# GpSimd additions ordered behind VectorE's port passes, later Q projections and two more weight buffers in a fused two-layer transformer kernel

## The chip, the cores and the metric

The kernel runs on one core of a Trainium2 chip. The metric is the device time of one execution in microseconds (us); lower is better. The engines are TensorE (PE in the profile, with its weight loads as PEld), VectorE (DVE), ScalarE (ACT), GpSimd (POOL) and SyncE (SP), which issues the DMAs.

## The reference

Two identical blocks follow each other, each with its own attention and its own dense part, on x of 2048 rows by 512 columns in bf16. Every matrix is the same in both blocks.

```python
def _A_ref(x, wqkv, wo):                      # 32 heads of 16 columns
    q, k, v = split(x @ wqkv)                 # [H, 2048, 16] each
    p = softmax(einsum("hqd,hkd->hqk", q, k) * 16 ** -0.5)
    return concat(einsum("hqk,hkd->hqd", p, v)) @ wo
def _B_ref(x, w1, b1, w2, b2):                # 512 -> 1792 -> 512
    return gelu(x @ w1 + b1) @ w2 + b2
for _ in range(2):
    x = x + _A_ref(layernorm(x), wqkv, wo)
    x = x + _B_ref(layernorm(x), w1, b1, w2, b2)
```

The softmax's 32 x 2048 x 2048 exponentials per layer are the bulk of the elementwise work.

## The kernel before, in words

Rows are cut into four chunks of 512 queries (the last chunk of layer 1 into two segments of 256). A *pass* is one group of four heads of one chunk over a range of the 16 key tiles of 128 rows. Its unit is a *cell*: the scores of one head's 512 columns against one key tile, [128, 512] in one PSUM bank. There are 4096 cells in the two layers.

A cell's exponential is taken in one of two ways. Most go to ScalarE (`exps`, L1751): one ACTIVATE with Exp reads two or three neighbouring banks (two or three cells) and writes bf16 units called `pt`, which lie in the ring of that name or in lent tensors (`kt`, `q`, `v`, `g`). The others, only for the key tiles listed in `KD`, go over VectorE and GpSimd (`join`, `dfirst`, `dchain`). VectorE evicts the bank with one TENSOR_SCALAR that turns the score into the bits of a bf16 power of two (L1507, into a `du` buffer, of which some lie in `kt` and `v`). GpSimd then makes three shifted copies by adding integers to those words: L1596 makes copy 1, L1598 copies 2 and 3, for one or two cells at once. The four copies are multiplied by V and by three scaled copies of V (`vc`, L1282), so that such a cell takes four products where ScalarE's takes one. `pvs` (L1817) does all these products.

Around the attention run, per chunk, the output projection (`wo`), a layernorm, the dense part (`hpair`, `gelu`, `ytile`), another layernorm, and the next layer's K, V and Q projections (`proj`, spawned by `projections`). A layernorm (`ln`, `ln_tile`) consists of statistics per tile, a row of very small VectorE instructions on [128, 1] to [128, 4] columns (VARR L739, RSTD L749 and L755, RA L752, RB L753, NMR L757), which form the inverse square root, and one pass per tile (XLN, L774). Q is masked per head pair into `qp` (L1299); the softmax division writes `ott` (L946).

Weights come in pieces of 256 KB into a pool of buffers `WR` (`wloads`, `wload`, L1035): four of its own, and for the last segment four more in layer 0's K (`wlate`). Every piece's buffer comes free when its last use is ordered, and the next load in a fixed list takes it. SyncE issues all DMAs in order.

Nothing is ordered by hand. `_Sched` runs all these generators against planned clocks of the engines and writes out one instruction list per engine; on the chip the lists run in order and semaphores keep the dependencies. The planner chooses, at each step, the ready operation with the earliest start. `_ready` adds one thing to the dependencies: an operation marked `port` (a VectorE instruction that reads and writes SBUF) is not planned to start inside a GpSimd addition, and the other way round. In the kernel before this is only in the planned times, and the mark is set by the name of what is written:

```python
self.port = eng == "dve" and ... self.writes[0].startswith(("OTT", "NMR", "QP", "VC", "XLN", "PT", "V0", "V1")) ...
if op.eng == "pool":
    at = max(t, self.clock["pool"])
    for a, b in self.port_ops[-4:]:
        if a <= at < b - HEAD:
            at = t = b - HEAD
```

When TensorE would wait, the planner fills in dummy matmuls (`filler`, L1339, and the zero products at L1825). `PICKS` chooses for each stretch of 24 planned microseconds one of the rows of constants in `ORDERS`, by which the planner decides.

Of the kernel before, what the change touches and what calls it, by code (L numbers as in the profile page):

```python
# [50 lines left out]
KD = ((4, 5, 6, 7, 8), (0, 1, 2, 8, 12))  # L51
NKD = 5
TAIL = 10
OPENING = 18
# [46 lines left out]
STRETCH = 24  # L101
PICKS = (3, 9, 9, 3, 3, 3, 9, 3, 1, 3, 3, 9, 9, 9, 1, 9, 9, 3, 9, 9, 5, 3, 3, 9,
         3, 9, 9, 9, 3, 1, 9, 9, 3, 9, 9, 9, 3, 3, 9, 3, 9, 3, 9, 9, 3, 5, 9, 5,
         1, 9, 9, 9, 9, 3, 9, 9, 5, 3, 4, 3)
LOG2E = 1.4426950408889634
# [114 lines left out]
class _Op:  # L220
    __slots__ = ("eng", "cost", "fns", "reads", "writes", "sem", "by", "tail", "prio", "mode", "slack", "late", "back", "port", "limit", "after")

    def __init__(self, eng, cost, fns, reads=(), writes=(), sem=None, by=1, tail=0.0, prio=None, mode="F", slack=None):
        self.eng, self.cost = eng, cost
        self.fns = fns if isinstance(fns, list) else [fns]
        self.reads, self.writes = list(reads), list(writes)
        self.sem, self.by, self.tail, self.prio, self.mode, self.slack = sem, by, tail, prio, mode, slack
        self.limit = 1e9
        self.late, self.after = None, []
        self.port = eng == "dve" and self.writes[:1] != [] and self.writes[0].startswith(("OTT", "NMR", "QP", "VC", "XLN", "PT", "V0", "V1")) and not self.reads[:1] == [] and not self.reads[0].startswith("B.")  # L230

# [19 lines left out]
class _Sched:  # L251
# [152 lines left out]
    def run(self):  # L404
        while True:
# [65 lines left out]
            if e == "dve" and op.port:  # L471
                self.port_ops.append((start, start + cost))
            if e == "pool" and op.writes[0] != "LIB":
                self.pool_ops.append((start, start + cost))


SW = 0.107
STEP = 0.01
DENSITY = {"S": 1.0, "P": 1.0, "F": 4.0}


def bass_interleave_layers__mha_block__dense_activation_gelu__prompt_kernel(
# [15 lines left out]
    with ExitStack() as es:  # L498
# [28 lines left out]
        if DU % 2:  # L527
# [30 lines left out]
        sem_names = ["pe", "act", "dve", "pool", "dxt0", "dxt1", "dxt2", "dxt3", "dx1", "dx2", "dx3", "dwq", "dwk", "dwv", "db1", "db2"] + ["dw%d" % c for c in range(3)] + [  # L558
                     "dout", "dk0", "dk1"] + ["dwr%d" % i for i in range(W_RING + W_MORE)] + ["dtr%d" % i for i in range(XLN_RING)]
        sems = {n: es.enter_context(nc.semaphore("s_" + n)) for n in sem_names}  # L560
# [36 lines left out]
class _Plan:  # L597
# [279 lines left out]
    def projections(self, l, c, prio):  # L877
# [115 lines left out]
    def wloads(self):  # L993
# [33 lines left out]
        for i, (piece, (src, n), uses) in enumerate(out):  # L1027
            if i == len(out) - (NFC // 2 + 1 - W_MORE):
                yield ("spawn", self.wlate(late), 3)
            w = yield ("acq", "w")  # L1030
            yield from self.wload(piece, src, n, uses, w, [])

    def wload(self, piece, src, n, uses, w, over):
# [424 lines left out]
    def scores(self):  # L1458
        u = 0
        pools = self.s.pools  # L1460
        while True:
# [25 lines left out]
            for d, b, pair, j in extra:  # L1487
                yield ("spawn", self.dfirst(pair, j, b), DPRIO)
                if j == 0:
# [14 lines left out]

    def dfirst(self, pair, j, b):
        u = self.T["DU"][pair["du"]][:, 0, j, :]
        yield _Op("dve", 0.682, lambda e: e.tensor_scalar(u, self.bank(b), E_SCALE, E_BIAS, op0=ALU.mult, op1=ALU.add),  # L1507
                  reads=["B.%d" % b], writes=["DU.%d.0.%d" % (pair["du"], j)] + self.over(pair["du"]))
        pair["done"] = pair.get("done", 0) + 1
        yield ("rel", "dbank", b)  # L1510

    def solo(self):
# [10 lines left out]
        while True:  # L1523
# [9 lines left out]
            d, b, pair, j = extra[0]  # L1533
            yield ("spawn", self.dfirst(pair, j, b), DPRIO)
            if j == 0:
# [42 lines left out]
    def dchain(self, pair):  # L1578
# [8 lines left out]
        yield ("cond", lambda: pair.get("done", 0) == len(cells))  # L1587
        n = len(cells)
        U = T["DU"][du]
        key = [["DU.%d.%d.%d" % (du, i, j) for j in range(n)] for i in range(4)]  # L1590
        def words(i, k):
# [4 lines left out]
        yield _Op("pool", 0.151 + 0.2176 * n, lambda e: e.int64_add(words(1, 1), words(0, 1), SHIFT * ONES),  # L1596
                  reads=key[0], writes=key[1])
        yield _Op("pool", 0.143 + 0.4352 * n, lambda e: e.int64_add(words(2, 2), words(0, 2), 2 * SHIFT * ONES),  # L1598
                  reads=key[0] + key[1], writes=key[2] + key[3])
        self.chains -= 1  # L1600
        self.duleft[du] = n
        for jj, (pi, kt, a) in enumerate(cells):
            l, seg, g = self.pas[pi][:3]
            gb, ts = self.heads(seg, g)
            j = KD[l].index(kt)
            for i in range(4):
                if i == 0:
                    ws, wk = [T["V"][l][:, kt, 8 * gb + 2 * a + t, 0:17] for t in ts], ["V%d.%d" % (l, kt), self.vone(l, kt)]
                else:
                    ws = [T["VC"][:, j, i - 1, 17 * h:17 * h + 17] for h in [8 * gb + 2 * a + t for t in ts]]  # L1610
                    wk = ["VC.%d.%d" % (j, i - 1)]
                self.dq[(pi, a)].append((ws, U[:, i, jj, :].bitcast(BF16), wk + [key[i][jj]],
                                         ("du", du) if i == 3 else None, i == 3, kt))

# [246 lines left out]
    def run(self):  # L1861
# [16 lines left out]
        s.spawn(self.loads(), 2)  # L1878
        s.spawn(self.init(), 3)
        s.spawn(self.wloads(), 3)  # L1880
        s.spawn(self.scores(), 0)
# [45 lines left out]
```

## Time and profile before

| | us |
|---|---|
| runs (three) | 1480.62, 1482.77, 1484.39 |
| median | 1482.77 |
| profiled execution, its own time | 1478.68 |
| span of the profile | 1476.7 |
| granted TensorE clock, mean | 0.999 |

| engine | busy us | share of the span | instructions |
|---|---|---|---|
| ACT | 1427.6 | 97% | 1422 |
| PE | 1415.5 | 96% | 19639 |
| DVE | 1219.1 | 83% | 2246 |
| POOL | 977.8 | 66% | 1235 |

The profile is of one execution. Busy time counts an instruction from its recorded start to its end; instructions that follow each other on ACT or DVE overlap in the record, so the mean of one is longer than its share of the busy time. PE's busy time holds the dummy matmuls. The span is 2.0 us shorter than the execution's own time, and that execution was 4.1 us faster than the median.

### The profile page before, as it was taken

Reading aid. Unit: us, or ns where it says so; the run is one execution under the profiler, and the core shown is the slowest. Engines: PE = TensorE matmul, PEld = TensorE weight load, DVE = VectorE, ACT = ScalarE, POOL = GpSimd, SP = SyncE. Lnnn points to the kernel's source line nnn. Section 1 sums busy time; section 2 is a strip of 40 time slices with the busy share of each in tenths; the row PEclk is TensorE's granted clock in tenths of the full one; section 3 lists DMA queues with packets and bytes.
Section 4 is the critical chain, followed back from the end, with each engine's and each line's share of the span. In section 5 each row is a group of like instructions: output and inputs, shape, how many; then the busy total and the mean of one; then the engine's idle time right before and its main releaser. Section 6 shows DMA issues by size and latency. Waiting matters only on the chain.

```text
span 1476.7 us, 45759 instructions
## 1 busy us (share of the span) xinstructions
PE 1415.5 (96%) x19639; PEld 428.0 (29%) x19639; DVE 1219.1 (83%) x2246; ACT 1427.6 (97%) x1422; POOL 977.8 (66%) x1235
## 2 busy tenths in 40 slices
PE   8999999999999999999999999999999999999999
PEld 3222222222222222222222222222222222334445
DVE  7768989878987789987797788999968987887683
ACT  7999999999999999999999999999999999999995
POOL 1057977867676777886556756667867876776661
PEclk9999999999999999999999999999999999999999
DMA  5200001153112521114320243101143115511533
GB/s 154 49 2 1 2 16 30 38 168 82 47 45 59 164 66 31 48 34 130 122 60 25 59 122 114 30 2 37 30 131 115 37 37 137 158 31 38 162 91 95
DMA packets 145045, 103.35 MB, mean 70 GB/s; under 512 B 37069, under 2 KB 143822, under 8 KB 144846
## 3 DMA queue, kind: packets, MB, share of 16 engines
q1 hardware_dynamic: 144846, 100.44, 24.6%
q8 instruction: 157, 2.57, 0.8%
q14 instruction: 42, 0.34, 0.1%
HBM read 88.61 MB, written 4.19 MB: 63 GB/s over the span
## 4 chain that ended last, share of the span: by engine, by line
ACT 52%; PE 30%; DVE 14%; DMA 1%; POOL 1%; issue 1%; SPq 0%; ACTq 0%; DVEq 0%
ACT pt L1751 41%; PE ps L607 10%; PE ps L1351 10%; PE ps L1817 9%; DVE du L1507 6%; ACT g L1102 3%; ACT kt L1751 2%; ACT q L1751 2%; ACT v L1751 2%; DVE kt L1507 1%; DVE v L1507 1%; DVE xln L774 1%; DVE stats L734 1%; DMA wr<-in_B_w_dram 1%; ACT L1102 1%
## 5 line engine op out<-in xcount | busy, mean ns | idle before, releaser
L1751 ACT ACTIVATE pt<-ps 128x1024 bf16<-128x1024 f32 (+1 forms) x1096 | 1103.9, 1136 | 18.2 <-PE ps L1351 12.0
L1507 DVE TENSOR_SCALAR du<-ps 128x512 uint16<-128x512 f32 x858 | 572.4, 683 | 115.9 <-PE ps L1351 112.3
L1351 PE MATMUL ps<-qp,kt 32*128 32x512 bf16 x4096 | 553.8, 384 | 37.4 <-ACT pt L1751 11.4
L1596 POOL INT64_ADD du<-du x444 | 266.9, 602 | 318.5 <-DVE du L1507 290.9
L1598 POOL INT64_ADD du<-du x444 | 449.1, 1013 | 35.5
L1817 PE MATMUL ps<-du,vc 128*17 128x512 bf16 (+1 forms) x2856 | 324.2, 360 | 1.4 <-ACT pt L1751 0.5
L1351 PEld LDWEIGHTS ps<-qp,kt 32*128 32x128 bf16 x4096 | 144.7, 91 | 601.3 <-issue 175.0
L1817 PE MATMUL ps<-pt,v 128*17 128x512 bf16 (+1 forms) x2630 | 283.9, 360 | 5.3 <-ACT pt L1751 2.1
L1507 DVE TENSOR_SCALAR kt<-ps 128x512 uint16<-128x512 f32 x200 | 134.7, 682 | 34.0 <-PE ps L1351 33.2
L1817 PE MATMUL ps<-du,v 128*17 128x512 bf16 (+1 forms) x952 | 142.4, 360 | 3.9 <-DVE xt L937 1.2
L1817 PE MATMUL ps<-kt,vc 128*17 128x512 bf16 (+1 forms) x714 | 136.3, 347 | 0.1
L607 PE MATMUL ps<-xf,wr 128*32 128x512 bf16 (+1 forms) x1888 | 131.0, 365 | 0.0
L607 PE MATMUL ps<-wr,g 128*32 128x512 bf16 x1600 | 118.9, 382 | 1.6 <-DMA wr<-in_B_w_dram 1.5
L1598 POOL INT64_ADD kt<-kt x104 | 105.1, 1011 | 8.3
L1817 PEld LDWEIGHTS ps<-du,vc 128*17 128x17 bf16 x2856 | 87.7, 89 | 75.3 <-issue 38.1
L1596 POOL INT64_ADD kt<-kt x104 | 62.4, 600 | 60.8 <-DVE kt L1507 57.4
L1817 PEld LDWEIGHTS ps<-pt,v 128*17 128x17 bf16 x2630 | 69.1, 88 | 87.7 <-issue 62.5
L1817 PE MATMUL ps<-v,vc 128*17 128x512 bf16 (+1 forms) x402 | 90.3, 350 | 0.0
L1081 DVE TENSOR_SCALAR g<-ps,hb1t 128x512 bf16<-128x512 f32 (+1 forms) x112 | 79.2, 708 | 12.7 <-PE ps L607 12.0
L1817 PE MATMUL ps<-kt,v 128*17 128x512 bf16 (+1 forms) x390 | 85.9, 360 | 1.6 <-DVE xt L937 1.3
L1507 DVE TENSOR_SCALAR v<-ps 128x512 uint16<-128x512 f32 x115 | 77.5, 682 | 11.9 <-PE ps L1351 11.6
L1751 ACT ACTIVATE kt<-ps 128x1024 bf16<-128x1024 f32 (+1 forms) x71 | 78.5, 1134 | 2.5 <-PE ps L1351 0.6
(108 smaller groups left out, 1555.4 us busy)
## 6 DMA issues: line engine op xcount, KB each, us to landing
wr<-in_B_w_dram SPq DMA_DIRECT2D x256, 256.0 KB, 2.9
wr<-in_A_wqkv_dram SPq DMA_DIRECT2D x24, 256.0 KB, 2.9
wr<-in_A_wo_dram SPq DMA_DIRECT2D x18, 256.0 KB, 3.1
x<-in_A_x_dram SPq DMA_DIRECT2D x7, 512.0 KB, 4.1
kept<-x SPq DMA_DIRECT2D x4, 512.0 KB, 2.9
x<-kept SPq DMA_DIRECT2D x4, 512.0 KB, 4.1
out_dram<-x SPq DMA_DIRECT2D x16, 128.0 KB, 2.6
g<-in_A_wqkv_dram SPq DMA_DIRECT2D x3, 512.0 KB, 6.0
```

The source lines that it names most:

```text
L607: return [lambda e, a=a: e.matmul(out[32 * a:32 * a + 32, :], lhsT=lhsT[:, 32 * a:32 * a + 32], rhs=rhs, start=start, stop=stop, tile_posi ...
L734: yield _Op("dve", 0.66, lambda e, t=t: e.bn_stats(T["STATS"][:, t, :], T["X"][:, t % XT, :]), reads=["X.%d" % (t % XT)], writes=["ST.%d" ...
L774: yield _Op("dve", 0.41, lambda e: e.tensor_scalar(xl, T["X"][:, t % XT, :], T["RSTD"][:, t:t + 1], T["NMR"][:, t:t + 1], op0=ALU.mult, op ...
L1081: yield _Op("dve", 0.21 + n / 966, lambda e, fc=fc, pb=pb: e.tensor_scalar(T["G"][:, fc, q], pb, T["HB1T"][:, fc:fc + 1], None, op0=ALU.ad ...
L1102: lambda e, g=g: e.activation(out=g, in_=g, func=ACT.Gelu_apprx_tanh), reads=gk, writes=gk, prio=2)
L1351: return (lambda e: e.matmul(o, lhsT=lhsT, rhs=rhs, start=True, stop=True, tile_position=(32 * a, 0)), ["K%d.%d.%d" % (l, gb, kt // 4), "Q ...
L1507: yield _Op("dve", 0.682, lambda e: e.tensor_scalar(u, self.bank(b), E_SCALE, E_BIAS, op0=ALU.mult, op1=ALU.add), reads=["B.%d" % b], writ ...
L1596: yield _Op("pool", 0.151 + 0.2176 * n, lambda e: e.int64_add(words(1, 1), words(0, 1), SHIFT * ONES), reads=key[0], writes=key[1])
L1598: yield _Op("pool", 0.143 + 0.4352 * n, lambda e: e.int64_add(words(2, 2), words(0, 2), 2 * SHIFT * ONES), reads=key[0] + key[1], writes=k ...
L1751: yield _Op("act", 0.065 + 0.4267 * n, lambda e, src=src, dst=dst: e.activation(out=dst, in_=src, func=ACT.Exp, scale=0.25), reads=["B.%d" ...
L1817: op.fns.append(lambda e, o=o, lhsT=q[0][0][m], rhs=q[0][1][:, n * m:n * m + n], a=a, st=st, sp=sp: e.matmul(o, lhsT=lhsT, rhs=rhs, start= ...
```

## The change

The change has four parts, and a fifth that the description leaves out.

1. The mark `port` is also set for VARR, RSTD, RA and RB. GpSimd's operations are planned behind the newest port pass that is planned to start no later than they do (`last`), and the GpSimd instruction now also waits on the chip, by semaphore, for that pass.
2. In layer 0 the Q projections of chunks 1, 2 and 3 are not spawned before 200, 240 and 280 cells have been scored, and each of a chunk's four eight cells after the one before.
3. `XP`, the transposed input of layer 1's projections, becomes two more weight buffers when the last of these projections is done. In `wlate` only the first piece carries the list of what it overwrites.
4. `PICKS` is another list, so that the whole order is another.
5. The products of a `du` cell are offered copy by copy: copy 0 when its eviction is ordered, the others when their addition is, where all four were offered after both additions.

```diff
-PICKS = (3, 9, 9, 3, 3, 3, 9, 3, 1, 3, 3, 9, ...
+PICKS = (3, 3, 3, 3, 3, 3, 3, 3, 3, 3, 3, 3, ...
+QAT = (0, 200, 240, 280)
+QSTEP = 8
...
-        self.port = ... startswith(("OTT", "NMR", "QP", "VC", "XLN", "PT", "V0", "V1")) ...
+        self.port = ... startswith(("OTT", "NMR", "QP", "VC", "XLN", "PT", "V0", "V1", "VARR", "RSTD", "RA", "RB")) ...
...
         if op.eng == "pool":
-            at = max(t, self.clock["pool"])
-            for a, b in self.port_ops[-4:]:
-                if a <= at < b - HEAD:
-                    at = t = b - HEAD
+            t = max(t, self.last(max(t, self.clock["pool"]))[0])
...
+    def last(self, at):
+        for a, b, ev in self.port_ops[:-9:-1]:
+            if a <= at + LEAN:                       # LEAN = 0.0
+                return b + LATENCY["dve"], ev
+        return 0.0, None
...
+            if e == "pool" and op.writes[0] != "LIB":
+                over = self.last(start)[1]
+                if over:
+                    self.P.wait("pool", *over)
             ev = self.P.group(e, op.fns, op.reads, op.writes, op.sem, op.by)
...
+        T["WR"] += [T["XP"][:, 2 * i:2 * i + 2, :].rearrange("p c f -> p (c f)") for i in range(2)]
...
+            if l == 0 and kind == "Q" and c > 0:
+                yield ("cond", lambda i=i: self.scored >= QAT[c] + QSTEP * i)
             yield ("spawn", self.proj(l, kind, i, c, src, skeys, ph, (kind, l, i, c)), p)
...
+    def wmore(self):
+        self.wover = {}
+        yield ("need", ("pfree", 0, self.segs[0][-1]))
+        for w in (W_RING + W_MORE, W_RING + W_MORE + 1):
+            self.wover[w] = ["XP.%d" % t for t in range(4)]
+            yield ("rel", "w", w)
...
-            yield from self.wload(piece, src, n, uses, W_RING + i, over)
+            yield from self.wload(piece, src, n, uses, W_RING + i, [] if i else over)
...
 # dfirst: after the eviction        self.copied(cell, pair["du"], j, 0)
 # dchain: after the first addition  self.copied(cells[jj], du, jj, 1)
 #         after the second          self.copied(cells[jj], du, jj, i)   for i in (2, 3)
+    def copied(self, cell, du, jj, i):               # one copy's product goes to the queue of pvs
...
+        self.dq[(pi, a)].append((ws, T["DU"][du][:, i, jj, :].bitcast(BF16), wk + ["DU.%d.%d.%d" % (du, i, jj)],
+                                 ("du", du) if i == 3 else None, i == 3, kt))
```

More of the change, by code (lines that the diff above doesn't have):

```diff
@@ L229, in __init__ @@
         self.late, self.after = None, []
-        self.port = eng == "dve" and self.writes[:1] != [] and self.writes[0].startswith(("OTT", "NMR", "QP", "VC", "XLN", "PT", "V0", "V1")) and not self.reads[:1] == [] and not self.reads[0].startswith("B.")
+        self.port = eng == "dve" and self.writes[:1] != [] and self.writes[0].startswith(("OTT", "NMR", "QP", "VC", "XLN", "PT", "V0", "V1", "VARR", "RSTD", "RA", "RB")) and not self.reads[:1] == [] and not self.reads[0].startswith("B.")
 class _Thread:
@@ L471, in run @@
             if e == "dve" and op.port:
-                self.port_ops.append((start, start + cost))
+                self.port_ops.append((start, start + cost, ev))
             if e == "pool" and op.writes[0] != "LIB":
@@ L477 @@
 SW = 0.107
+LEAN = 0.0
 STEP = 0.01
@@ L558, in bass_interleave_layers__mha_block__dense_activation_gelu__prompt_kernel @@
         sem_names = ["pe", "act", "dve", "pool", "dxt0", "dxt1", "dxt2", "dxt3", "dx1", "dx2", "dx3", "dwq", "dwk", "dwv", "db1", "db2"] + ["dw%d" % c for c in range(3)] + [
-                     "dout", "dk0", "dk1"] + ["dwr%d" % i for i in range(W_RING + W_MORE)] + ["dtr%d" % i for i in range(XLN_RING)]
+                     "dout", "dk0", "dk1"] + ["dwr%d" % i for i in range(W_RING + W_MORE + 2)] + ["dtr%d" % i for i in range(XLN_RING)]
         sems = {n: es.enter_context(nc.semaphore("s_" + n)) for n in sem_names}
@@ L1030, in wloads @@
             w = yield ("acq", "w")
-            yield from self.wload(piece, src, n, uses, w, [])
+            yield from self.wload(piece, src, n, uses, w, self.wover.pop(w, []))
     def wload(self, piece, src, n, uses, w, over):
@@ L1487, in scores @@
             for d, b, pair, j in extra:
-                yield ("spawn", self.dfirst(pair, j, b), DPRIO)
+                yield ("spawn", self.dfirst(d, pair, j, b), DPRIO)
                 if j == 0:
@@ L1503, in scores, with dfirst @@
             yield ("rel", "misc", b)
-    def dfirst(self, pair, j, b):
+    def dfirst(self, cell, pair, j, b):
         u = self.T["DU"][pair["du"]][:, 0, j, :]
@@ L1508, in dfirst @@
                   reads=["B.%d" % b], writes=["DU.%d.0.%d" % (pair["du"], j)] + self.over(pair["du"]))
+        self.copied(cell, pair["du"], j, 0)
         pair["done"] = pair.get("done", 0) + 1
@@ L1533, in solo @@
             d, b, pair, j = extra[0]
-            yield ("spawn", self.dfirst(pair, j, b), DPRIO)
+            yield ("spawn", self.dfirst(d, pair, j, b), DPRIO)
             if j == 0:
@@ L1588, in dchain @@
         n = len(cells)
+        self.duleft[du] = n
         U = T["DU"][du]
@@ L1597, in dchain @@
                   reads=key[0], writes=key[1])
+        for jj in range(n):
+            self.copied(cells[jj], du, jj, 1)
         yield _Op("pool", 0.143 + 0.4352 * n, lambda e: e.int64_add(words(2, 2), words(0, 2), 2 * SHIFT * ONES),
                   reads=key[0] + key[1], writes=key[2] + key[3])
+        for i in (2, 3):
+            for jj in range(n):
+                self.copied(cells[jj], du, jj, i)
         self.chains -= 1
[L1601 to L1604, printed above, removed]
-            j = KD[l].index(kt)
[L1606 to L1613, printed above, removed]
+    def copied(self, cell, du, jj, i):
+        T = self.T
+        pi, kt, a = cell
+        l, seg, g = self.pas[pi][:3]
+        gb, ts = self.heads(seg, g)
+        hs = [8 * gb + 2 * a + t for t in ts]
+        if i == 0:
+            ws, wk = [T["V"][l][:, kt, h, 0:17] for h in hs], ["V%d.%d" % (l, kt), self.vone(l, kt)]
+        else:
+            j = KD[l].index(kt)
+            ws, wk = [T["VC"][:, j, i - 1, 17 * h:17 * h + 17] for h in hs], ["VC.%d.%d" % (j, i - 1)]
+        self.dq[(pi, a)].append((ws, T["DU"][du][:, i, jj, :].bitcast(BF16), wk + ["DU.%d.%d.%d" % (du, i, jj)],
+                                 ("du", du) if i == 3 else None, i == 3, kt))
     def units(self, n):
```

7 lines of the change are left out of this document (4 added, 3 removed).

## The prediction

> **What bounds the kernel now.** I read the page's busy times first, then ScalarE's groups by form, the windows of 50 us, ScalarE's waits, and at last the timeline around those waits.
>
> ```profile
> span 1476.7 us, 45759 instructions
> ## 1 busy us (share of the span) xinstructions
> PE 1415.5 (96%) x19639; PEld 428.0 (29%) x19639; DVE 1219.1 (83%) x2246; ACT 1427.6 (97%) x1422; POOL 977.8 (66%) x1235
> ...
> L1507 DVE TENSOR_SCALAR du<-ps 128x512 uint16<-128x512 f32 x858 | 572.4, 683 | 115.9 <-PE ps L1351 112.3
> ...
> L1596 POOL INT64_ADD du<-du x444 | 266.9, 602 | 318.5 <-DVE du L1507 290.9
> ```
>
> ScalarE is idle for 1476.7 − 1427.6 = 49.1 us only. PE's 96% has dummy matmuls in it, GpSimd has 1476.7 − 977.8 = 498.9 us to spare, and most of VectorE's and GpSimd's idle time ends with work arriving. So the end is set by how long ScalarE's exponentials take, and by its gaps. The next rows are ScalarE's groups by form: two cells, three cells, one cell.
>
> ```profile
> L1751 ACT ACTIVATE pt<-ps 128x1024 bf16<-128x1024 f32 x924 | 888.1, 1068 | 15.7 <-PE ps L1351 10.7 <-PE ps L1817 4.1
> L1751 ACT ACTIVATE pt<-ps 128x1536 bf16<-128x1536 f32 x171 | 248.3, 1508 | 2.5 <-PE ps L1351 1.3 <-PE ps L1817 0.9
> ...
> L1751 ACT ACTIVATE pt<-ps 128x512 bf16<-128x512 f32 x1 | 0.6, 607 | 0.0
> ```
>
> The means (1068, 1508 ns) hold the overlap with the next instruction; what one takes of the busy time is 888.1/924 = 0.961 us for two cells and 248.3/171 = 1.452 us for three. These are the prices I use.
>
> **Part 1: the opening.** Two windows of 50 us (columns: length, then busy us and instructions of PE, PEld, DVE, ACT, POOL; clock; DMA):
>
> ```profile
> 50.00:100.00 50.00, 49.08 (x621) 13.43 (x621) 31.52 (x54) 48.82 (x49) 13.22 (x16) 1.00 0.08 20
> 100.00:150.00 50.00, 48.46 (x623) 13.03 (x623) 43.39 (x74) 50.00 (x50) 39.34 (x49) 1.00 0.01 2
> ```
>
> From 50 to 100 us VectorE is busy for 31.52 of 50 and GpSimd for 13.22, while ScalarE is full: the second way of taking a cell is hardly in use, since the K, V and Q projections hold PE and the banks. The order of the two built kernels, without any time, shows what moves. In the old order layer 0's last K or V eviction stands after 191 scored cells and the twelve Q evictions of chunks 1 to 3 between 65 and 245; in the new one after 143, and between 209 and 338. Each moved projection issues its 16 matmuls and one VectorE eviction, no DMA; chunk 1's Q is first read by passes that begin after 512 cells, so 512 − 338 = 174 cells are still in hand, and what comes next in its place are the K and V projections. Of cells 129 to 256, 30 go to VectorE in the old order and 39 in the new one; over the first 640 cells it is 160 against 170.
>
> Over the whole kernel VectorE takes 1185 cells against 1173, ScalarE 2911 against 2923. ScalarE's instructions become 1169 of two cells (1164 before), 191 of three (198) and none of one (1). By the prices above: 5 × 0.961 − 7 × 1.452 − 0.6 = −6.0 us. The gelus, and with them the table loads, stay 16, in adjacent pairs. As ScalarE is full in this stretch, I take all of it: **−6.0 us**. Against it stand 12 × 0.683 = 8.2 us more of VectorE, ten of these cells where it has 50 − 31.5 us free in one window; if that cover were gone, they would come back as 0 to +8.2 us of late evictions. I take 0.
>
> **Part 2: GpSimd behind VectorE's passes.** What the two do to each other is seen in the timeline from 224 us on:
>
> ```profile
> 224.66 0.17 DVE L752 TENSOR_TENSOR ra<-rstd 128x4 f32<-128x4 f32 x1
> 224.75 1.22 DVE L1299 TENSOR_SCALAR qp<-q,mask 128x512 bf16<-128x512 bf16 x1
> ...
> 224.79 2.08 POOL L1598 INT64_ADD du<-du  x2
> ...
> 225.90 0.99 DVE L753 SCALAR_TENSOR_TENSOR rb<-ra,varr 128x4 f32<-128x4 f32 x1
> ...
> 228.96 0.40 PE L1351 MATMUL ps<-qp,kt 32*128 32x512 bf16 x4 [1.19 <-DVE kt L1507]
> ...
> 229.40 1.02 ACT L1751 ACTIVATE pt<-ps 128x1024 bf16<-128x1024 f32 x1 [1.26 <-PE ps L1351]
> ```
>
> GpSimd runs two additions from 224.79 to 226.87. VectorE's `qp` pass ends only after the first, and the four-column RB, no larger than the RA of 0.17 us in the first row, ends at 226.89 with the second. The evictions behind them are late, PE waits 1.19 us for a bank, ScalarE 1.26 us for PE. RB has no `port` mark in the old planner, so the plan did not know of its 0.99 us. The sizes by form:
>
> ```profile
> L752 DVE TENSOR_TENSOR ra<-rstd 128x2 f32<-128x2 f32 x18 | 7.0, 391 | 0.4 <-DVE rstd L755 0.2
> ...
> L755 DVE SCALAR_TENSOR_TENSOR rstd<-rb,rstd 128x2 f32<-128x2 f32 x18 | 5.8, 321 | 0.4
> ...
> L753 DVE SCALAR_TENSOR_TENSOR rb<-ra,varr 128x4 f32<-128x4 f32 x20 | 5.1, 257 | 0.1
> L752 DVE TENSOR_TENSOR ra<-rstd 128x4 f32<-128x4 f32 x20 | 5.1, 258 | 0.1
> L755 DVE SCALAR_TENSOR_TENSOR rstd<-rb,rstd 128x4 f32<-128x4 f32 x20 | 4.7, 235 | 0.1
> L753 DVE SCALAR_TENSOR_TENSOR rb<-ra,varr 128x2 f32<-128x2 f32 x18 | 4.6, 253 | 0.5 <-DVE ra L752 0.3
> ```
>
> The RA at 224.66 shows what an undisturbed one takes: 0.17 us. The six unmarked groups are 114 instructions and 32.3 us; undisturbed they would be 114 × 0.17 = 19.4. So 12.9 us of VectorE's time is delay that the old plan did not hold. In the new order 185 of the additions wait for a port pass: 70 for a `qp` pass, 34 for `ott`, 24 for `xln`, 50 for one of the newly marked small ones, 7 for others. Whatever of these VectorE has ordered ahead goes first, and GpSimd, with 498.9 us spare, waits; behind it in its queue stand only further additions, and those who wait for them are the products of copies 1 to 3.
>
> How much of that reaches ScalarE? Its waits, first from 222 to 232 us, then (two rows) from 100 to 1440 us:
>
> ```profile
> ACT pt L1751 <- PE ps L1351: 2.3, 3, 1.3
> ```
>
> ```profile
> ACT pt L1751 <- PE ps L1351: 12.0, 24, 1.3
> ACT pt L1751 <- PE ps L1817: 4.1, 2, 2.9
> ```
>
> In the 10 us around the case shown it waits three times, 2.3 us in all, always for L1351. The upper end is all of the two long rows, −16.1 us; the lower end is no gain, and a loss if GpSimd's waits make new gaps (below). Evictions that come late through the port end in waits for L1351, as at 229.40; those for L1817 are another kind. In front of most of the longer gaps the timeline has a stretched small pass as it has here, though not of all: I take 60% of the 12.0 us for L1351, 0.6 × 12.0 = **−7.2 us**, nearer to the stretch shown, where it is all of it, than to nothing.
>
> The Trainium skill, page "SBUF — State Buffer", section "Who interferes with whom", says that VectorE and GpSimd share a port pair as an exclusive lock: whoever starts first holds it for the whole instruction, and the other fully blocks. The trace agrees: RB's 0.99 us ends with GpSimd's addition. By that rule alone no port time is saved, it is only given to the other side, and the sum would be the −6.0 of the cells; that is the second rival.
>
> **Parts 3 to 5.** 42 of the 298 loads into `WR` go to `XP`. What weights cost PE (waits), and the kernel's last stretch (the chain that ended last):
>
> ```profile
> PEld ps L607 <- DMA wr<-in_B_w_dram: 3.5, 7, 1.2
> ```
>
> ```profile
> 1459.84 14.03 PE ps L607 x368
> ```
>
> PE's 3.5 us of waiting for weights is spread over the span and lies beside dummy matmuls; the end (14.03 us of PE without a wait for a DMA in it) needs no buffer earlier. On SP's queue the transposes L778 stand behind fewer loads that wait for a buffer. 0, at best −1.7 (half). The early offer of copy 0 adds no product; it only lets PE fill earlier: 0, hidden by GpSimd's addition that the last copy waits for anyhow. The new picks can move gaps anywhere; of them I know the counts above alone, and bound them by the two rows of ScalarE's waits, from −16.1 (with part 2) to one more wait of the longest kind, +2.9; I take 0.
>
> Sum: −6.0 − 7.2 = −13.2 us. Against the profiled execution's own 1478.68 that is 1465.5; against the median, 4.1 us higher, 1482.77 − 13.2 = **1469.6 us**.
>
> **The rivals.**
>
> *Slower: GpSimd's waits come back through the products.* GpSimd is in order. If the pass that it waits for is itself queued behind an eviction that waits for PE, every later addition is late, then the products of those copies, then the `pt` units they share PE's queue with. The old trace has one such case:
>
> ```profile
> 412.45 0.61 POOL L1596 INT64_ADD du<-du  x1 [1.97 <-DVE du L1507]
> ...
> 414.66 1.02 ACT L1751 ACTIVATE pt<-ps 128x1024 bf16<-128x1024 f32 x1 [2.86 <-PE ps L1817]
> ```
>
> One costs ScalarE 2.86 us. The forecast is used up at 13.2/2.86 = 4.6 of them. At one in thirty of the 185 waits there are six, 17.2 us; if the gaps of part 2 stay as well, −6.0 + 17.2 = +11.2, 1494.0. Against it: only two of ScalarE's waits from 100 to 1440 us are for L1817, and GpSimd is 66% busy. Chance 0.14.
>
> *The delay only changes sides.* Two additions and two passes want the same stretch from 224.79 to 226.89, and will still want it. VectorE's 12.9 us go to GpSimd, which then returns `du` buffers later by as much, and the gaps stay. Only the cells count: 1482.77 − 6.0 = 1476.8. For it: nothing is made shorter. Against it: GpSimd has the spare time and VectorE's evictions hold the banks. Chance 0.19. The skill's rule above is this case.
>
> *The cells are paid back.* The 8.2 us of evictions come at ScalarE's cost where VectorE is dense, and no gap closes: the 6.0 us return, 1482.8. Against it are the 18 free us of the window from 50 to 100. Chance 0.12.
>
> *More than forecast.* All gaps of the two rows close and the weights' half comes too: −6.0 − 16.1 − 1.7 = −23.8, 1459.0. Chance 0.05; the forecast has 0.50.
>
> **How the numbers follow.** The range goes from 1459.0, the upper end of every term, to the case without gain and one stall of 2.86 us more, 1485.6; only most of the slower rival is outside. A measurement of this kernel tells some 0.3%, 4.4 us, from no change, so faster means under 1478.3. Faster: 0.50 + 0.05 and three quarters of the second rival, 0.14: 0.69. Same: the rest of it and the third rival, 0.17. Slower: 0.14.
>
> **What would show it.** Right: groups RA, RB and RSTD near 0.15 to 0.2 us a piece; ScalarE's wait for L1351 near 5 us between 100 and 1440; GpSimd's idle time now ended by `qp`, `ott`, `ra` and `rb` passes; more GpSimd work in the window from 50 to 100 us; ScalarE's busy time near 1421.6. Wrong: ScalarE waiting for L1817 more than twice, for several us (first rival); small passes short but the L1351 waits unchanged (second); a span that shrinks by less than ScalarE's busy time (third).

## The result, and the profile after

The changed kernel takes 1457.56 us (median of four runs, 1456.55 to 1458.49) against 1481.69 us (four runs, 1479.82 to 1484.39): a ratio of 0.9836, 95% interval 0.9817 to 0.9854. That is 24.1 us where 13.2 were forecast, and 1.4 us under the low end of the range. Beside the experiments below the kernel before had medians of 1479.2 to 1480.0 us, so some 2 us of the 24 may belong to those first runs. The profiled execution of the changed kernel took 1458.49 us.

The page's first part, then ScalarE's two large groups by form, then its waits from 100 to 1440 us, all of the changed kernel (L1779 is L1751 before, L1371 is L1351, L1845 is L1817):

```profile
span 1456.7 us, 45980 instructions
...
PE 1412.3 (97%) x19676; PEld 430.4 (30%) x19676; DVE 1208.5 (83%) x2258; ACT 1419.9 (97%) x1419; POOL 981.3 (67%) x1239
```

```profile
L1779 ACT ACTIVATE pt<-ps 128x1024 bf16<-128x1024 f32 x948 | 908.0, 1066 | 9.6 <-PE ps L1371 4.5 <-PE ps L1845 3.9
L1779 ACT ACTIVATE pt<-ps 128x1536 bf16<-128x1536 f32 x166 | 240.2, 1514 | 0.3 <-PE ps L1371 0.2
```

```profile
ACT pt L1779 <- PE ps L1371: 4.7, 13, 0.6
ACT pt L1779 <- PE ps L1845: 3.9, 1, 3.9
```

ScalarE's busy time falls by 7.7 us (6.0 forecast) and its idle time from 49.1 to 36.8 us, 12.3 us. The waits for score matmuls fall from 12.0 to 4.7 us, as forecast. For products it waited twice there, 4.1 us, and now waits once, 3.9 us; that is another wait, at 580.75 us where the longer of the old two was at 414.66. The window from 50 to 100 us now has GpSimd busy for 27.23 us where it was 13.22, and VectorE for 37.77 where it was 31.52:

```profile
50.00:100.00 50.00, 48.30 (x634) 13.33 (x635) 37.77 (x64) 50.00 (x49) 27.23 (x34) 1.00 0.10 22
```

The six small groups that the prediction counted (two columns and four columns of RA, RB, RSTD):

```profile
L764 DVE SCALAR_TENSOR_TENSOR rb<-ra,varr 128x2 f32<-128x2 f32 x18 | 5.2, 290 | 0.2
...
L766 DVE SCALAR_TENSOR_TENSOR rstd<-rb,rstd 128x2 f32<-128x2 f32 x18 | 4.4, 246 | 0.2
L763 DVE TENSOR_TENSOR ra<-rstd 128x4 f32<-128x4 f32 x20 | 4.3, 217 | 0.1
L764 DVE SCALAR_TENSOR_TENSOR rb<-ra,varr 128x4 f32<-128x4 f32 x20 | 4.3, 215 | 0.2
L766 DVE SCALAR_TENSOR_TENSOR rstd<-rb,rstd 128x4 f32<-128x4 f32 x20 | 3.9, 196 | 0.1
L763 DVE TENSOR_TENSOR ra<-rstd 128x2 f32<-128x2 f32 x18 | 3.5, 197 | 0.3
```

Together 25.6 us where they were 32.3: only 6.7 of the 12.9 us of delay are gone, one of these instructions takes 0.196 to 0.290 us and not the 0.15 to 0.2 that the prediction named, and yet the kernel gained more than forecast. The experiments look for the rest.

### The profile page after: what moved, and what is told of

Same layout as the page of the kernel before. It is cut to its first block, busy times and chain, and to the rows that moved or that the text cites. A ratio compares the mean times of both kernels' runs of the same rounds, so it can differ in the third digit from the quotient of the medians.

```text
span 1456.7 us, 45980 instructions
## 1 busy us (share of the span) xinstructions
PE 1412.3 (97%) x19676; PEld 430.4 (30%) x19676; DVE 1208.5 (83%) x2258; ACT 1419.9 (97%) x1419; POOL 981.3 (67%) x1239
## 4 chain that ended last, share of the span: by engine, by line
ACT 48%; PE 40%; DVE 11%; issue 1%; DMA 0%; POOL 0%; POOLq 0%; ACTq 0%
ACT pt L1779 37%; PE ps L1845 13%; PE ps L1371 13%; PE ps L618 12%; DVE du L1527 4%; ACT g L1122 3%; ACT kt L1779 2%; ACT q L1779 2%; ACT v L1779 1%; DVE kt L1527 1%; PE ps L1359 1%; ACT L1779 1%; ACT L1122 1%; DVE xln L785 1%; DVE xt L950 1%
## 5 line engine op out<-in xcount | busy, mean ns | idle before, releaser
L1779 ACT ACTIVATE pt<-ps 128x1024 bf16<-128x1024 f32 (+1 forms) x1114 | 1117.5, 1133 | 9.9 <-PE ps L1371 4.7
L1527 DVE TENSOR_SCALAR du<-ps 128x512 uint16<-128x512 f32 x873 | 580.3, 683 | 111.1 <-PE ps L1371 106.9
L1371 PE MATMUL ps<-qp,kt 32*128 32x512 bf16 x4096 | 549.5, 385 | 19.7 <-ACT pt L1779 12.2
L1622 POOL INT64_ADD du<-du x448 | 455.4, 1018 | 58.1 <-DVE qp L1319 10.0
L1618 POOL INT64_ADD du<-du x448 | 268.5, 600 | 269.4 <-DVE du L1527 218.7
L1845 PE MATMUL ps<-du,vc 128*17 128x512 bf16 (+1 forms) x2913 | 335.1, 361 | 2.8 <-POOL du L1622 1.1
L1371 PEld LDWEIGHTS ps<-qp,kt 32*128 32x128 bf16 x4096 | 142.8, 91 | 573.1 <-issue 177.0
L1845 PE MATMUL ps<-pt,v 128*17 128x512 bf16 (+1 forms) x2678 | 299.7, 360 | 4.8 <-ACT pt L1779 2.9
L1845 PE MATMUL ps<-du,v 128*17 128x512 bf16 (+1 forms) x971 | 152.1, 362 | 4.4 <-DVE xt L950 1.3
L1845 PE MATMUL ps<-kt,vc 128*17 128x512 bf16 (+1 forms) x693 | 138.3, 348 | 0.9 <-POOL du L1622 0.4
L1845 PEld LDWEIGHTS ps<-du,vc 128*17 128x17 bf16 x2913 | 91.8, 89 | 80.0 <-issue 37.6
L1622 POOL INT64_ADD kt<-kt x102 | 102.1, 1001 | 14.6 <-DVE qp L1319 2.5
L618 PE MATMUL ps<-xf,wr 128*32 128x512 bf16 (+1 forms) x1504 | 107.7, 372 | 0.9 <-DMA xf<-xln 0.9
L618 PE MATMUL ps<-wr,g 128*32 128x512 bf16 x1368 | 100.8, 382 | 0.4 <-ACT g L1122 0.3
L1845 PEld LDWEIGHTS ps<-pt,v 128*17 128x17 bf16 x2678 | 73.8, 88 | 88.4 <-issue 56.5
L1101 DVE TENSOR_SCALAR g<-ps,hb1t 128x512 bf16<-128x512 f32 (+1 forms) x112 | 79.1, 708 | 15.9 <-PE ps L618 15.8
L1845 PE MATMUL ps<-kt,v 128*17 128x512 bf16 (+1 forms) x355 | 84.7, 360 | 1.1 <-POOL du L1618 0.6
L1779 ACT ACTIVATE q<-ps 128x1024 bf16<-128x1024 f32 (+1 forms) x80 | 84.5, 1107 | 1.2 <-PE ps L1371 1.1
L1845 PE MATMUL ps<-v,vc 128*17 128x512 bf16 (+1 forms) x411 | 83.8, 350 | 1.0 <-POOL du L1622 0.7
```

Source lines behind the costliest of these rows:

```text
L618: return [lambda e, a=a: e.matmul(out[32 * a:32 * a + 32, :], lhsT=lhsT[:, 32 * a:32 * a + 32], rhs=rhs, start=start, stop=stop, tile_posi ...
L1101: yield _Op("dve", 0.21 + n / 966, lambda e, fc=fc, pb=pb: e.tensor_scalar(T["G"][:, fc, q], pb, T["HB1T"][:, fc:fc + 1], None, op0=ALU.ad ...
L1371: return (lambda e: e.matmul(o, lhsT=lhsT, rhs=rhs, start=True, stop=True, tile_position=(32 * a, 0)), ["K%d.%d.%d" % (l, gb, kt // 4), "Q ...
L1779: yield _Op("act", 0.065 + 0.4267 * n, lambda e, src=src, dst=dst: e.activation(out=dst, in_=src, func=ACT.Exp, scale=0.25), reads=["B.%d" ...
L1845: op.fns.append(lambda e, o=o, lhsT=q[0][0][m], rhs=q[0][1][:, n * m:n * m + n], a=a, st=st, sp=sp: e.matmul(o, lhsT=lhsT, rhs=rhs, start= ...
```

## The experiments

Each was timed in at least three rounds beside the kernel before on the same chip; the ratio is to that. "Stream ends" is when the last exponential ends in the profiled execution, "rest" the span after it. "Score" and "product" are the sums of ScalarE's waits for the score matmuls and for the products. The kernels with an asterisk run in exactly the instruction order of another one.

| kernel | us | ratio, 95% interval | VectorE's cells | stream ends | rest | score | product |
|---|---|---|---|---|---|---|---|
| before | 1481.69 | | 1173 | 1448.8 | 27.9 | 15.5 | 5.2 |
| after | 1457.56 | 0.9836 [0.9817, 0.9854] | 1185 | 1429.3 | 27.3 | 6.3 | 3.9 |
| after, no waits* | 1476.53 | 0.9978 [0.9965, 0.9990] | 1185 | 1448.4 | 27.3 | 18.0 | 3.9 |
| before, waits added* | 1479.28 | 0.9996 [0.9987, 1.0006] | 1173 | 1450.5 | 27.9 | 17.0 | 5.2 |
| after, waits for small passes* | 1472.56 | 0.9947 [0.9930, 0.9965] | 1185 | 1443.7 | 28.0 | 15.8 | 3.9 |
| after, waits for large passes* | 1461.59 | 0.9873 [0.9856, 0.9889] | 1185 | 1433.6 | 27.1 | 8.9 | 3.9 |
| after without the port part | 1488.80 | 1.0061 [1.0041, 1.0081] | 1176 | 1458.0 | 28.2 | 17.0 | 11.8 |
| before + port part | 1485.22 | 1.0042 [1.0027, 1.0057] | 1158 | 1448.6 | 35.1 | 6.6 | 10.1 |
| before + Q late | 1481.16 | 1.0009 [1.0000, 1.0019] | 1183 | 1446.8 | 33.5 | 14.7 | 9.1 |
| before + port + Q late | 1480.22 | 1.0004 [0.9995, 1.0014] | 1180 | 1430.1 | 47.2 | 2.4 | 6.8 |
| ... + buffers | 1470.59 | 0.9942 [0.9927, 0.9956] | 1173 | 1434.6 | 33.7 | 3.4 | 6.8 |
| ... + early copies (= after, old picks) | 1473.20 | 0.9958 [0.9942, 0.9975] | 1171 | 1438.4 | 33.2 | 4.0 | 8.9 |
| after, Q early | 1477.55 | 0.9987 [0.9978, 0.9996] | 1162 | 1447.4 | 27.8 | 4.5 | 14.4 |
| after, no more buffers | 1463.41 | 0.9892 [0.9872, 0.9913] | 1182 | 1428.8 | 31.5 | 4.6 | 3.9 |
| after, copies late | 1472.18 | 0.9958 [0.9944, 0.9972] | 1169 | 1439.3 | 29.7 | 2.7 | 10.4 |
| after, picks all alike | 1464.24 | 0.9892 [0.9871, 0.9913] | 1185 | 1430.8 | 28.9 | 2.7 | 8.6 |
| picks alike, no waits* | 1483.04 | 1.0027 [1.0016, 1.0039] | 1185 | 1451.7 | 28.6 | 18.4 | 8.6 |

### The waits, in fixed orders

The changed kernel without the semaphore waits, everything else as it was:

```diff
-            if e == "pool" and op.writes[0] != "LIB":
-                over = self.last(start)[1]
-                if over:
-                    self.P.wait("pool", *over)
```

> The changed kernel in exactly its order, without the semaphore waits of GpSimd for VectorE's port passes. Theory A (the waits themselves, by which the chip keeps the planned sequence of port holders, bring most of what was not forecast): some 8 to 12 us of the 24.1 us are lost, about 1466 to 1470 us, with a wider spread, and ScalarE's waits for L1355 (the score matmuls) go back towards 12 us. Theory B (the new order is better in itself, and the waits hardly matter): 1457 to 1459 us.

1476.53 us: the waits are worth 19.0 us in this order, about twice what theory A gave them. The two kernels were not timed side by side, and the kernel before differed by 2.2 us between the two occasions (1481.69, 1479.51), so the figure is good to about that; the two profiled spans differ by 19.0 us as well. Four rows of the timeline without them, and the same place with them:

```profile
218.72 2.05 POOL L1618 INT64_ADD du<-du  x2
218.78 0.99 DVE L762 SCALAR_TENSOR_TENSOR rstd<-rb,rstd 128x4 f32<-128x4 f32 x1
219.70 1.22 DVE L1315 TENSOR_SCALAR qp<-q,mask 128x512 bf16<-128x512 bf16 x1
...
222.58 1.45 ACT L1775 ACTIVATE pt<-ps 128x1536 bf16<-128x1536 f32 x1 [1.70 <-PE ps L1367]
```

```profile
216.93 0.20 DVE L766 SCALAR_TENSOR_TENSOR rstd<-rb,rstd 128x4 f32<-128x4 f32 x1
217.05 0.34 DVE L1319 TENSOR_SCALAR qp<-q,mask 128x512 bf16<-128x512 bf16 x1
...
217.49 1.04 POOL L1622 INT64_ADD du<-du  x1 [0.38 <-DVE qp L1319]
...
219.05 1.45 ACT L1779 ACTIVATE pt<-ps 128x1536 bf16<-128x1536 f32 x1 [0.23 <-PE ps L1371]
```

Without the wait the additions begin 0.06 us before RSTD and hold it for 0.99 us, then `qp` for 1.22, and the exponential of three cells waits 1.70 us. With it GpSimd waits 0.38 us, the two passes take 0.20 and 0.34, and ScalarE waits 0.23. The Trainium skill, page "SBUF — State Buffer", section "Who interferes with whom", says it so: "Issue order, not op shape, decides who blocks." The trace agrees: the same instructions in the same lists took 1.22 and 0.34 us. (`qp`'s recorded start, 219.70, lies inside RSTD, which ends at 219.78; the second of the two additions starts at 219.74, so `qp` is read here as the one that came second.)

The large passes of VectorE, by line, first of the kernel before, then of the changed order without waits, then of the changed kernel:

```profile
L1299 DVE TENSOR_SCALAR qp<-q,mask 128x512 bf16<-128x512 bf16 (+1 forms) x103 | 47.2, 458 | 9.2 <-PE ps L1351 8.9
L946 DVE TENSOR_TENSOR ott<-xt,rc 128x256 bf16<-128x256 f32 (+1 forms) x72 | 39.7, 556 | 1.2
L774 DVE TENSOR_SCALAR xln<-x,rstd,nmr 128x512 bf16<-128x512 bf16 x60 | 31.0, 533 | 2.4 <-DMA kt<-xln 2.0
```

```profile
L1315 DVE TENSOR_SCALAR qp<-q,mask 128x512 bf16<-128x512 bf16 (+1 forms) x103 | 48.5, 471 | 5.7 <-PE ps L1367 5.4
L955 DVE TENSOR_TENSOR ott<-xt,rc 128x256 bf16<-128x256 f32 (+1 forms) x72 | 45.4, 639 | 1.2
L781 DVE TENSOR_SCALAR xln<-x,rstd,nmr 128x512 bf16<-128x512 bf16 x60 | 31.2, 543 | 2.4 <-DMA kt<-xln 1.9
```

```profile
L959 DVE TENSOR_TENSOR ott<-xt,rc 128x256 bf16<-128x256 f32 (+1 forms) x72 | 40.0, 563 | 1.2
L1319 DVE TENSOR_SCALAR qp<-q,mask 128x512 bf16<-128x512 bf16 (+1 forms) x103 | 38.8, 377 | 6.2 <-PE ps L1371 5.9
L785 DVE TENSOR_SCALAR xln<-x,rstd,nmr 128x512 bf16<-128x512 bf16 x60 | 27.2, 477 | 2.6 <-DMA kt<-xln 2.0 <-DMA xf<-xln 0.2
```

They add up to 117.9, 125.1 and 106.0 us. In one order the waits shorten them by 19.1 us, and the six small groups by 6.3 (31.9 to 25.6). These large ones had the `port` mark already: the plan knew of the conflict, but without the waits the chip did not keep to the plan.

The kernel before in its own order, with the same kind of wait:

```diff
+            if e == "pool" and op.writes[0] != "LIB":
+                for at, over in self.locks[:-9:-1]:   # all marks, the four new ones too
+                    if at <= start:
+                        self.P.wait("pool", *over)
+                        break
```

> The kernel before in exactly its order, with GpSimd waiting for the newest port pass planned to start before it, the four small kinds included. Theory A: 6 to 10 us faster than before, about 1472 to 1476 us, and a narrower spread. Theory B: within 0.3% of before, or slower, since the plan held other times: 1479 to 1486 us.

No gain: 1479.28 us, score waits 17.0. Theory A fails here. Waits by themselves, in an order that was planned without them, pay nothing. They also shorten little there: the large passes take 111.8 us where they took 117.9, the six small groups 33.6 where they took 32.3. Why so little was not followed further. What did change is the spread, ten runs within 1478.11 to 1480.15 us where 31 of the kernel before lie within 1477.13 to 1482.68.

Which passes the 19.0 us belong to: the changed order with only one kind of the waits.

```diff
-                if over:
+                small = over in self.smalls        # VARR, RSTD, RA, RB
+                if over and small:                 # the other run: not small
                     self.P.wait("pool", *over)
```

> The changed kernel in exactly its order; of GpSimd's 185 waits only the 50 for the newly marked small passes (VARR, RSTD, RA, RB) are kept. Theory E (the size that the prediction missed lies in the large passes, qp, ott and xln, which the old plan knew but the chip did not keep to): most of the 19 us stay lost, 1469 to 1474 us. Rival, the prediction's own step (the small passes are what matters): 1458 to 1463 us.

> The changed kernel in exactly its order; of GpSimd's 185 waits only the 135 for qp, ott, xln and the few others are kept, the 50 for the small passes are not. Theory E: most of the 19 us are kept, 1460 to 1465 us. Rival (the small passes): 1466 to 1473 us.

1472.56 with the 50 waits for small passes, 1461.59 with the 135 for large ones: 4.0 and 14.9 us of the 19.0. Theory E holds. The passes go with it: the large ones take 127.0 us with the small waits alone and 106.8 with the large ones alone. ScalarE's first wait rows from 100 to 1440 us, of the order without waits, with those for small passes, with those for large ones:

```profile
ACT pt L1775 <- PE ps L1367: 16.3, 34, 1.7
```

```profile
ACT pt L1783 <- PE ps L1375: 14.5, 25, 1.8
```

```profile
ACT pt L1783 <- PE ps L1375: 7.9, 21, 1.1
```

Does what the waits are worth hang on the tuned picks? The changed kernel with all picks alike, and that order again without the waits:

```diff
-PICKS = (3, 3, 3, 3, ...
+PICKS = (3,) * 60
```

> The changed kernel with one and the same pick for all stretches; the planner makes another order, with the same 1185 cells for VectorE and the same ScalarE instructions by form. Theory C (a plan that the chip can keep is worth the time whatever the picks): within 4 us of the changed kernel, 1457 to 1462 us. Theory B (the list of picks is what fits this order, and any other order meets new waits for units): 1466 us or more, with ScalarE waiting for the products (L1843 or near it) several times for 2 to 5 us.

> The same order as in the run with all picks alike, without GpSimd's semaphore waits for VectorE's port passes. Theory C (the waits keep the chip to a plan that counts on them): again 10 to 20 us slower than with them. Rival (the 19 us that the waits were worth belong to the one tuned order): less than 5 us.

1464.24 and 1483.04 us: 18.8 us for the waits once more, in another order, as theory C had it. Between these two lists of picks the waits are worth the same. The tuned picks themselves are worth 6.7 us against the plain list, between the two theories. ScalarE waits 4.7 us longer for products with the plain list (8.6 against 3.9) and 3.6 us less for scores (2.7 against 6.3).

### One part at a time

Everything but the port part, with the old marks, the old rule and no waits:

> All of the change but the port part: old marks, old planning of GpSimd, no waits; VectorE takes 1176 cells, ScalarE's exponentials are 4.4 us more by the prices of the prediction. Theory F (plan and waits only work together; each alone is worth nothing): like the changed order without the waits, 1474 to 1482 us, ScalarE's waits for score matmuls at 14 us or more. Rival (the other parts carry a good share by themselves): 1470 us or less.

1488.80 us, slower than the kernel before, with score waits of 17.0 us and product waits of 11.8. That is on theory F's side and beyond its figure: in this one order the other parts by themselves carry nothing of the gain. The changed order without the waits, which has the port part's plan but not its waits, is 12.3 us faster than this one. That lies in fewer product waits (3.9 against 11.8) and more cells on VectorE (4.4 us by the prices), not in the score waits, which are 18.0 us there.

From the kernel before upwards: the port part alone; the later Q projections alone; both.

```diff
 # port part: the four marks, last() and its wait, as shown under "The change"
...
+            if l == 0 and kind == "Q" and c > 0:                            # Q late
+                yield ("cond", lambda i=i: self.scored >= QAT[c] + QSTEP * i)
```

> The kernel before with part 2 alone: the four new marks, GpSimd planned behind port passes and waiting for them. VectorE takes 1158 cells (1173 before), ScalarE's exponentials are 7.1 us more by the prices of the prediction. Theory C (a plan that the chip keeps is worth some 18 us of ScalarE's stream): the stream of exponentials ends some 8 to 14 us earlier than before's 1448.8 us, about 1435 to 1441; the time depends on the last dense part, 1463 to 1485 us. Theory B (part 2 does not pay by itself): the stream ends at 1446 us or later.

> The kernel before with the later Q projections alone; the planner makes another order: 170 of the first 640 cells go to VectorE (160 before) and 1183 in all (1173). ScalarE's exponentials are 4.7 us less by the prices of the prediction. Theory A: 4 to 6 us faster than before, about 1476 to 1478 us. Theory B: the old picks no longer fit the order, so within 3 us of before or slower.

> The kernel before with two parts of the change together: the four new marks, GpSimd planned behind port passes and waiting for them on the chip, and the later Q projections. Old picks, no further weight buffers, no early offer of copies. VectorE takes 1180 cells; ScalarE's exponentials are 3.6 us less than before's by the prices of the prediction. Theory C: 3.6 us and some 10 us of waits less, 1464 to 1468 us. Theory B: within 5 us of before, 1475 to 1481 us.

1485.22, 1481.16 and 1480.22 us: theory B each time, the first by the end of its stream (1448.6), the others by their times. The port part alone does cut the score waits to 6.6 us, but the stream ends where it did. In the third, with 2.4 us, the stream of exponentials ends at 1430.1, 18.7 us before the old one, as far as in the changed kernel. All of it is lost behind the stream, which is 47.2 us from the end where it was 27.9. ScalarE's first wait there, and the same place in its timeline:

```profile
ACT g L1114 <- DVE g L1093: 18.6, 2, 15.0
```

```profile
1426.32 3.74 ACT L1763 ACTIVATE pt<-ps 128x1536 bf16<-128x1536 f32 x3
1430.08 1.28 ACT L1114 ACT_TABLE_LOAD   x1
1446.38 1.70 ACT L1114 ACTIVATE g<-g 128x1792 bf16<-128x1792 bf16 x1 [15.02 <-DVE g L1093]
```

The exponentials are done, and the GELU of the last segment but one waits 15 us for its dense part, which the planner had not placed earlier; why it did not stays open. In the port part alone there are 15 cells fewer on VectorE (7.1 us by the prices of the prediction), 4.9 us more of product waits and 7.2 us more behind the stream, against 8.9 us of score waits less. That adds up to 10.3 us where the span grew by 7.0, since ScalarE's busy time rose by only 4.2 and not by 7.1.

Then the buffers, and with them the early copies:

```diff
+        s.spawn(self.wmore(), 3)                      # both runs
+        self.copied(cell, pair["du"], j, 0)           # the second run, with the calls in dchain
```

> The kernel before with the port part, the later Q projections and the two further weight buffers; old picks, copies offered late. VectorE takes 1173 cells. Theory D (the buffers are what lets the last dense part end in time): the stream ends near 1433 us and what comes after it falls from 47 us to 28 to 32: 1462 to 1467 us. Rival (the buffers are worth some 4 us, as the changed kernel without them showed, and something else held the last dense part): 40 us or more after the stream, 1474 us or more.

> All of the change but the picks. VectorE takes 1171 cells, ScalarE's exponentials are 6.8 us more than the changed kernel's by the prices of the prediction. Theory C: like the order with all picks alike, which lost 6.7 us: 1462 to 1468 us. Theory B (the picks carry the gain): 1472 us or more.

With the buffers the rest behind the stream falls from 47.2 to 33.7 us, and the time by 9.6 us to 1470.59, between theory D and its rival. The early copies on top bring nothing with the old picks, in the order that comes of them: 1473.20. From there to the changed kernel are the picks alone, 15.6 us, which is theory B's figure for them.

From the changed kernel downwards: without the later Q projections, without the buffers, without the early copies.

> The changed kernel without the later Q projections of chunks 1 to 3; the planner makes another order from it: VectorE takes 162 of the first 640 cells where the change has 170, and 1162 in all against 1185. By ScalarE's prices that is 11 us of exponentials more. Theory A: 1457.6 + 11 = 1468 to 1469 us, by the cells alone. Theory B (the order as a whole, with its picks, is what was tuned, and any other order loses): 1470 us or more.

> The changed kernel without the two further weight buffers; the order differs, in its later part above all. VectorE takes 1182 cells, ScalarE's exponentials are 1.5 us more. Theory C: the buffers themselves are worth 0 to 2 us, so 1459 to 1461 us. Theory B: the picks do not fit the later part any more, 1465 us or more.

> All of the change but the early offer of copies. VectorE takes 1169 cells, ScalarE's exponentials are 7.8 us more by the prices of the prediction. Theory C: the early offer is worth nothing but these cells: 1463 to 1468 us, the stream ending near 1437 us. Rival (the early offer keeps the products from gathering at the end): more than 35 us after the stream, or ScalarE waiting for products for over 10 us in all; 1470 us or more.

1477.55, 1463.41 and 1472.18 us: 20.0, 5.9 and 14.6 us lost. The first and the third are theory B's and the rival's figures, the second lies between the two. For the first, 23 cells fewer on VectorE (11.3 us by the prices), 10.5 us more of product waits and 1.8 us less of score waits make 20.0. That it comes out so exactly is in part chance: ScalarE's busy time is 9.0 us more, not 11.3, and the profiled spans differ by 18.5. ScalarE's rows of it and of the third, from 100 to 1440 us:

```profile
ACT pt L1777 <- PE ps L1843: 8.6, 5, 3.0
ACT pt L1777 <- PE ps L1851: 4.6, 1, 4.6
```

```profile
ACT pt L1776 <- PE ps L1842: 10.4, 6, 2.6
```

The buffers show behind the stream, 31.5 us against 27.3. What stays open is how much of the 14.6 us of the early copies, and of the product waits in any of these, is the part and how much the draw of a new order: each edit makes the planner write another one, and each was tried in one order.

## Why the prediction was wrong

The direction was right. So was the mechanism of part 2 in the main, GpSimd made to wait so that VectorE's passes are not held up; where the delay sat and what it costs were not, and the time lies 1.4 us under the range. Of the 12.0 us between 1469.6 and 1457.56, 1.1 to 3.3 lie in the start of the sum: 1482.77 was the median of three executions, while four beside the changed kernel had a median of 1481.69 and 31 later ones 1479.51. The rest, 8.8 to 11.0 us, is in the terms.

*Part 1, the cells, −6.0.* The cells came as counted, and GpSimd's work in the window from 50 to 100 us doubled. ScalarE's busy time fell by 7.7 us, near the 6.0, but that is in part luck: in the same order without the waits, with the same cells, it is 1424.8 us, 2.8 less than before, and that kernel was 3.0 us faster than before (1476.53 against 1479.51). The other 4.9 us came with the waits. The prices were also somewhat high. The two groups by form and the single cell have 888.1 + 248.3 + 0.6 = 1137.0 us, but the page of the kernel before has the three together with 1103.9, so each group's time holds overlap with the others:

```profile
L1751 ACT ACTIVATE pt<-ps 128x1024 bf16<-128x1024 f32 (+1 forms) x1096 | 1103.9, 1136 | 18.2 <-PE ps L1351 12.0
```

In that trace, where the next exponential follows closely, it starts 0.904 us after one of two cells and 1.330 us after one of three (medians); with these prices the term is −5.4. And the cells are not worth their price in every order: alone, the later Q projections gave 1183 cells and no time, since 3.9 us went to product waits and 5.6 behind the stream.

*Part 2, −7.2.* This is the step that failed, by its size. The term was 60% of the 12.0 us that ScalarE is listed as waiting for L1351, with the two long rows of waits together, −16.1, as its upper end. In the fixed new order the waits are worth 19.0 us, more than that upper end. Two things were wrong in it.

The first is where the delay sat. It was counted over the newly marked small passes (12.9 us), and the 60% went by stretched small passes in front of the gaps, though the case shown had `qp`, a large pass with an old mark, at 1.22 us. No delay of these large passes stands in the working of the term. The old plan did count them, but the chip did not run as planned, and the large passes carry 14.9 of the 19.0 us, the small ones 4.0.

The second is that listed waits are no measure of what late work costs ScalarE. With and without the waits the same 1419 instructions leave 36.8 and 50.9 us of idle time, 14.1 us apart, and the busy time differs by another 4.9 us. An exponential of two cells is recorded as some 1.06 us long, but the next one can start 0.904 us after it did; where it starts a little later, the short gap counts as busy time. Of the 19.0 us only 11.7 are listed as score waits.

The term also had a condition that the sum did not name. In the old order the waits are worth nothing (1479.28 against 1479.51), and the whole port part put on the old kernel cost time; the 19.0 and the 18.8 us were measured in orders that had been planned for the waits.

That the score waits would come down to about 5 us was right: 4.7.

*Parts 3 to 5, 0.* Wrong as single terms, as far as one order each can tell. The buffers were judged by PE's 3.5 us of waits for weights; taken out or put in they move 5.9 and 9.6 us, most of it behind the stream (31.5 against 27.3 us, 47.2 against 33.7). The picks, taken as 0, are worth 6.7 us against the plain list and 15.6 against the old one.

*The sum.* I added parts that do not add. Put on the kernel before, the port part alone costs 3.5 us or more, the late Q projections alone give nothing, and both together end the stream 18.7 us early only to wait for a GELU.

*The rivals.* The delay did change sides, as the second rival said: with the waits GpSimd's idle time before its second additions grew by 22.9 us, from 35.2 to 58.1, where VectorE's passes became 25.4 us shorter. But the gaps did not stay, and the kernel was 19.0 us faster. The first row is the changed order without waits, the second the changed kernel:

```profile
L1618 POOL INT64_ADD du<-du x448 | 457.1, 1022 | 35.2
```

```profile
L1622 POOL INT64_ADD du<-du x448 | 455.4, 1018 | 58.1 <-DVE qp L1319 10.0 <-DVE ott L959 5.3 <-DVE xln L785 5.2
```

GpSimd's waits did not come back through the products: ScalarE waits for products 3.9 us, once, in the changed order with and without the waits. The cells were not paid back in this order; with the later Q projections alone they were.

## What to carry to other kernels

A planned conflict is only avoided if the chip is made to keep the plan: where two engines share something, let the planner count it and let a semaphore fix who goes first, and give the wait to the engine with idle time. Neither half paid much here without the other: 1479.28 us with waits that the old order was not planned for, 1476.53 with the changed kernel's plan and no waits, 1457.56 with both. Both halves were not enough either: on the old kernel, with the old picks, they shortened the passes and the score waits but took 1485.22 us, because that order lost as much elsewhere. Judge such a change only with the rest of the order fitted to it. When the stream that sets the end gets shorter, look at once at what runs behind it: 18.7 us gained in the exponentials were worth nothing while the last dense part kept its place.

## What the runs showed that was not expected

In two fixed orders the time itself seems to vary less with the waits: 1478.11 to 1480.15 us over ten runs of the old order, against 1477.13 to 1482.68 over 31 without; the changed order without them spreads from 1472.8 to 1480.7 over ten, and with them from 1456.55 to 1458.49 over four; the counts are unequal, and a range grows with its count. It is not so in every order: ten runs of the kernel before with the later Q projections spread over 3.3 us without waits, and ten with the port part added, waits included, over 4.4. Who comes first at the port by a tenth of a microsecond differs from run to run, or so it seems; the profiles hold one execution each and cannot show it.

In nine orders planned with the port rule and run with all the waits, ScalarE's score waits are 2.4 to 6.6 us; in the five without, 14.7 to 18.4. No other part of the change moves this number as far.
